# Second DFT in mirrored pairs, modulation rows in quadrants, shared check tiles: one change to a spectral mixing block with an MLP

## The chip, the cores and the metric

The kernel runs on one core of a Trainium2 chip. The metric is the device time of one execution in microseconds, as the median of several runs. The core has a matrix engine (PE, with a separate row PEld for the loading of weights), a vector engine (DVE), a scalar engine (ACT), a general engine (POOL) and an engine that only issues transfers (SP). Transfers can be issued by SP or by POOL; each of these queues issues in order, and an issue may wait for a semaphore.

## The reference

`x` is 2048 tokens of 1024 features. Six rows of 1024 numbers, `sa, ca, ga, sb, cb, gb`, come from one product of `silu(c)` with `w_mod` (1024 × 6144), and modulate two blocks:

```python
h = _layernorm(x) * (1 + ca) + sa
a, b = h @ hid_re.T, h @ hid_im.T             # first DFT, over the 1024 features
x = x + ga * (seq_re @ a - seq_im @ b)        # second DFT, over the 2048 tokens
h = _layernorm(x) * (1 + cb) + sb
x = x + gb * (gelu(h @ w1 + b1) @ w2 + b2)    # MLP, 1024 -> 3584 -> 1024
```

The four DFT matrices are inputs. All is float32.

## The kernel before

The kernel assumes that the DFT matrices have the symmetries of a DFT, works with folded (even and odd) sums and small parts of the matrices, and checks the assumption while it runs: all of both pairs of matrices is read, compared with itself mirrored or shifted, and the squares of the differences are summed. A verdict comes near the end; if it is bad, a general version runs after the fast one. Large products are done in float16, each operand split into a high and a low part, with three passes (high·high, high·low, low·high).

The program is written by a planner. Work is handed to it as tasks in named streams, each with an engine, an estimated cost, keys that it needs and a due time. The planner keeps a modelled clock for every engine and picks, among the tasks at the heads of the streams, by due time and by which can start first. So the order of an engine's instructions follows from costs and due times, and a changed cost may move work far away. The stages are:

- Modulation (`mod_part` and what follows, lines 2538 to 2598). Two of the six rows, `sa` and `ca`, are needed first. The eight pieces of `w_mod` are loaded by SP (L2504). Pieces 0, 1, 3 and 5 are multiplied on PE with a broadcast column of `silu(c)`, so that every output partition holds the row (L2556, four banks of 512); pieces 2, 4, 6 and 7 are multiplied and added on DVE (L2540, L2542) and reduced by four last PE products. DVE takes the largest value of each bank (L2568), ACT copies the row (L2582), PE turns it into columns by products with a 1 × 1 operand (L2588), and DVE scales these (L2592).
- The first LayerNorm (BN_STATS L2646, ACT L2676) on 16 tiles of 128 tokens, transposes on PE (L2693), and sums and differences of mirrored features (L2706, L2710, L2711, L2761 to L2788).
- The four remaining rows (`row`, L2900): per row 16 products of 128 × 512, broadcast to all output partitions. Rows `ga`, `cb` and `sb` come during the folds, `gb` late, in the stage of the second LayerNorm.
- First DFT (L2969), then the second DFT in `seq_tile(i)` for 16 tiles of 128 tokens: a product Q of 12 or 13 matmuls of 512 columns (L3058), a product P of 24 or 26 of 256 or 257 columns (L3046), a copy of Q by ACT (L3063), and `P - Q` and `P + Q` for the lower and upper columns by DVE (L3068, L3073). Tiles 4 to 7 of each half use negated copies of two parts of the matrix (`neg_tasks`, ACT L3015).
- Second LayerNorm in pairs of tiles (`ln2(b)`, b = 0 to 7). For b = 0, 6 and 7 `x` is loaded beside (L3101) and added by DVE (L3138, L3139); for b = 1 to 5 an accumulating transfer of POOL adds `x` (L3145) to what DVE made (L3143). The sum is stored (L3148), squared by ACT, and the reciprocal root taken by ACT (L2620) and DVE (L2626 to L2629); two scalings by DVE (L3158, L3162), a shift by DVE (L3169) and ACT (L3171). Then PE transposes (`turn`, L3181), ACT copies the result into a single buffer (L3185), and the pieces of `z` (L3211, L3220, L3233) become the first MLP operand.
- The MLP: products of the first layer (L3628) and the second (L3742). Groups of 12 products of the first two blocks (`gemm3_first`) are put into gaps of PE before the last transposes. The checks run beside the MLP: loads by POOL (L3559, with lists of rows L3552), differences by DVE (L3542), squares by ACT (L3533).

Weights `w1` and `w2` are also folded and split by DVE and ACT (L2379, L2391, L2405) and stored to memory in float16 (for `w1`'s first three blocks by POOL); loads of `fw` bring them back.

## Time and profile before

| | us |
|---|---|
| three runs | 1371.27, 1367.63, 1370.13 |
| median | 1370.13 |
| span of the profiled execution | 1368.1 |
| PE busy in the span | 1285.2 |
| DVE busy | 1089.1 |
| ACT busy | 748.2 |
| POOL busy | 263.8 |

The profile is of one execution, and its span lies within the three runs. Busy shares are means over the whole span; the stages above have different limits, so the prediction reads them by stretches of time. In a row of the timeline stand start, length, engine and line, operation, output and input, and in brackets the idle time before and what ended it. In a group of instructions stand the count, the busy time, the mean in ns, and the idle time just before them.

### The profile page before, as it was taken

The numbers are of one execution on the slowest core, as the hardware profiler recorded it, in microseconds if no ns is written. First come the engines' busy times: TensorE is split into PE (matmuls) and PEld (weight loads), VectorE is DVE, ScalarE is ACT, GpSimd is POOL, SyncE is SP. The second block draws the span as 40 slices with busy tenths as digits, with TensorE's granted clock in tenths as the row PEclk, the third lists the DMA queues.
The fourth block names the chain that finished last, engine by engine and source line by source line (L and its number), as shares of the span: only waits on it lengthen the run. The fifth ranks groups of instructions, "written<-read, shape, count | busy, mean of one in ns | idle before, by whom it ended". The sixth has DMA issues, their size and how long they took to land.

```text
span 1368.1 us, 17330 instructions
## 1 busy us (share of the span) xinstructions
PE 1285.2 (94%) x6081; PEld 620.1 (45%) x6081; DVE 1089.1 (80%) x1623; ACT 748.2 (55%) x1188; POOL 263.8 (19%) x426
## 2 busy tenths in 40 slices
...
GB/s 367 335 249 210 1 171 168 146 196 341 245 150 217 261 197 228 181 228 157 158 173 139 193 246 193 283 338 351 244 320 233 300 268 294 264 307 235 175 80 112
DMA packets 109753, 306.21 MB, mean 224 GB/s; under 512 B 14076, under 2 KB 14076, under 8 KB 107736
## 3 DMA queue, kind: packets, MB, share of 16 engines
...
q8 instruction: 49, 0.80, 0.2%
...
## 4 chain that ended last, share of the span: by engine, by line
PE 67%; DVE 10%; DMA 3%; ACT 2%; issue 2%; SPq 1%; POOL 0%; DVEq 0%; POOLq 0%; ACTq 0%
PE ps L3742 34%; PE ps L3628 31%; DVE arena L2391 2%; DVE arena L3220 1%; DVE arena L3162 1%; DVE arena L2405 1%; ACT arena L2379 1%; DMA arena<-in_w_dram 1%; PE ps L3046 1%; DVE arena L3233 1%; DMA arena<-in_wm_dram 1%; PE ps L3058 1%; DMA frow_gbb<-arena 0%; DVE arena L3654 0%; PE ps L3181 0%
## 5 line engine op out<-in xcount | busy, mean ns | idle before, releaser
L3628 PE MATMUL ps<-arena 128*128 128x512 f16 x2352 | 515.1, 381 | 9.7 <-DMA arena<-fw 5.4
L3742 PE MATMUL ps<-arena 128*128 128x512 f16 x2352 | 510.7, 379 | 4.9 <-DVE arena L3792 4.2
L3628 PEld LDWEIGHTS <-arena 128*128 128x128 f16 x2352 | 230.8, 98 | 290.2 <-issue 9.6
L3742 PEld LDWEIGHTS <-arena 128*128 128x128 f16 x2352 | 229.8, 98 | 283.5 <-DVE arena L3792 3.2
L3792 DVE SCALAR_TENSOR_TENSOR arena<-ps,i4c,arena 128x1024 f32<-128x1024 f32 x179 | 229.4, 1282 | 103.0 <-PE ps L3742 101.0
L2379 ACT ACTIVATE arena<-arena,shc 128x512 f16<-128x512 f32 (+1 forms) x115 | 116.0, 1017 | 134.4 <-DVE arena L2405 81.5
L2405 DVE TENSOR_TENSOR arena<-arena 128x512 f32<-128x512 f32 (+1 forms) x196 | 148.9, 764 | 3.7
L2391 DVE SCALAR_TENSOR_TENSOR arena<-arena,shc 128x512 f16<-128x512 f32 (+1 forms) x115 | 128.8, 1121 | 28.2 <-ACT arena L2379 27.8
L3533 ACT ACTIVATE arena<-arena 128x512 f32<-128x512 f32 (+5 forms) x148 | 91.2, 617 | 108.7 <-DVE arena L3542 89.8
L3647 ACT ACTIVATE arena<-arena,b1s,i1c 128x512 f32<-128x512 f32 x78 | 63.5, 814 | 94.4 <-DVE arena L3654 94.4
L3654 DVE TENSOR_TENSOR arena<-arena,ps 128x512 f32<-128x512 f32 x78 | 53.4, 685 | 51.6 <-PE ps L3628 50.9
L2379 ACT ACTIVATE arena<-arena,s1c 128x512 f16<-128x512 f32 (+1 forms) x70 | 60.7, 885 | 56.9 <-DVE arena L2405 39.6
L3542 DVE TENSOR_TENSOR arena<-arena 128x256 f32<-128x256 f32 x240 | 87.9, 420 | 1.8 <-DMA arena<-in_cre_dram 1.8
...
L3559 POOL DMA_DIRECT2D arena<-in_cim_dram x99 | 54.5, 551 | 92.3 <-ACT arena L3533 86.4
L2391 DVE SCALAR_TENSOR_TENSOR arena<-arena,s1c 128x512 f16<-128x512 f32 (+1 forms) x70 | 65.7, 958 | 2.9 <-ACT arena L2379 2.8
L3559 POOL DMA_DIRECT2D arena<-in_cre_dram x99 | 54.6, 552 | 68.3 <-ACT arena L3533 51.5
L3650 ACT ACTIVATE arena<-ps 128x512 f32<-128x512 f32 x78 | 45.9, 589 | 37.5 <-PE ps L3628 37.3
L2900 PE MATMUL ps<-arena,scol 128*128 128x512 f32 x128 | 61.5, 630 | 2.7 <-DMA arena<-in_wm_dram 2.4
L2391 DVE SCALAR_TENSOR_TENSOR arena<-arena,s2c 128x1024 f16<-128x1024 f32 x49 | 61.8, 1278 | 1.0 <-ACT arena L2379 1.0
L3046 PE MATMUL ps<-arena 128*128 128x256 f16 (+3 forms) x400 | 50.5, 286 | 10.1 <-DVE arena L3073 10.1
L3311 ACT ACTIVATE ps<-arena 128x1024 f32<-128x1024 f32 x46 | 46.7, 1016 | 19.0 <-DMA arena<-in_w_dram 9.6
...
## 6 DMA issues: line engine op xcount, KB each, us to landing
fw<-arena SPq DMA_DIRECT2D x71, 512.0 KB, 5.1
arena<-fw SPq DMA_DIRECT2D x119, 256.0 KB, 5.0
arena<-fw SPq DMA_DIRECT2D x49, 512.0 KB, 6.2
arena<-in_cre_dram POOLq DMA_DIRECT2D x96, 256.0 KB, 5.5
arena<-in_cim_dram POOLq DMA_DIRECT2D x96, 256.0 KB, 5.3
arena<-in_wm_dram SPq DMA_DIRECT2D x32, 512.0 KB, 6.8
arena<-in_w_dram SPq DMA_DIRECT2D x32, 512.0 KB, 6.2
arena<-in_w_dram SPq DMA_DIRECT2D x56, 256.0 KB, 4.7
```

Of the source, the lines that this page charges most:

```text
L2379: act.activation(o[m][0], q(j), AF.Copy, **sc)
L2391: dve.scalar_tensor_tensor(o[m][1], q(j), scale, o[m][0], op0=ALU.mult, op1=ALU.subtract)
L2405: dve.tensor_tensor(q(d), q(a), q(b), op=op)
L2900: pe.matmul(bank((6 if n < 3 else 4) + h), scol[:, k : k + 1].to_broadcast([P, P]), FA(o + 512 * h, (1, 512)), start=k == 0, stop=k == 7,)
L3046: pe.matmul(PA(pb + o, (1, w)), l, r, start=n == 0, stop=n == len(mm_) - 1)
L3533: f = lambda: act.activation(sq(a), sq(a), AF.Square, accum_out=csum[0:pn, n : n + 1])
L3542: dve.tensor_tensor(a[:, o::2], a[:, o::2], b[:, o::2], op=op)
L3559: return lambda t: gp.dma_start(t[0:pn], v)
L3628: pe.matmul(ps.rearrange("p (k t) -> p k t", k=4), w1c[:, m, s, a, d * P : (d + 1) * P], zc(m)[:, b, :, d, :], start=(start and d == 0 and ...
L3647: act.activation(dst, src, AF.Gelu_apprx_tanh, scale=inv, bias=b1s[:, 2 * p + j : 2 * p + j + 1])
L3742: pe.matmul(t[:, j], hidc[:, c_, m, a, k * P : (k + 1) * P], w2c[:, m, c_, w], start=(start and c_ == 0 and n == 0), stop=(c_ == 1 and n = ...
L3792: lambda: dve.scalar_tensor_tensor(dst, ps[b], inv, dst, op0=ALU.mult, op1=ALU.add), kp[b],
```

## The change

It does six things.

- Second DFT: `seq_pair(b)` takes the place of two `seq_tile`s. One P and one Q give both tiles of a pair, since a mirrored token has the same real row read backwards in the features. `up` is 257 columns wide, and LN2 reads the second tile through `yr`, an access with negative step. Only the tile with token 0 needs a further product of one output row (26 matmuls) and three ACT copies. `neg_tasks` is gone. The tokens of the second tile are the mirrored ones, so they are loaded, added and stored with lists of rows (`mirrored`, `from_rows`, `to_rows`, all on POOL): one load each for b = 0, 6 and 7, five accumulating loads, eight stores, four accumulating stores at the end.
- Modulation rows in quadrants: the products for the first rows write 32 output partitions each, four pieces of 512 columns at four places of the same bank, for all eight pieces of `w_mod`. DVE's multiply-adds are gone, one maximum and an all-reduce on POOL take the place of four maxima, four transposes that of 34 small products. The rows of `row` become 16 quarter products, a copy and two products that sum the quarters. `gb` is made in the middle of the second DFT, not late.
- x tiles 4 to 7 are loaded ahead of the eight pieces of `w_mod`.
- A second buffer for the transposed tiles (`ZT0`), used in turn until b = 5.
- The first MLP products and some weight loads wait for other keys (`zlo`, P and Q of earlier pairs).
- Checks share tiles (`fetch`, `chk`): a tile that is compared several times is loaded once; 76 fewer transfers of 256 KB. Differences, squares and the verdict stay.

The core of the diff:

```diff
+    def mirrored(v, h, k):
+
+        return v[0:1024], bass.IndirectOffsetOnAxis(ap=idx_m[:, 4 * h + k : 4 * h + k + 1], axis=0)
+
+    def last_rows(blk, r, hf):
+
+        c_ = slice(512 * hf, 512 * hf + 512)
+        return [o_s[1, 3 - 2 * blk - j if r else 4 + 2 * blk + j, :, c_] for j in range(2)]
+
+    def from_rows(dst, rows, idx, **op):
+        gp.indirect_dma_start(out=dst, out_offset=None, in_=rows, in_offset=idx, **op)
+
+    def to_rows(rows, idx, src, **op):
+        gp.indirect_dma_start(out=rows, out_offset=idx, in_=src, in_offset=None, **op)
...
     for i in range(4):
         load_x(i)
     load_raw1(0)
+    for i in range(4, 8):
+        load_x(i)
     for k in range(8):
         load(("wm", k), lambda k=k: sp.dma_start(wm2(k), wm[:, k, 0 : 2 * D]), cost=2.75)
-    for i in range(4, 8):
...
-        if k in (2, 4, 6, 7):
...
+            if k == 0:
+                for q in (2, 3):
+                    pe.matmul(quarter(VB, q, 512), ones[0:1, 0:32], ones[0:1, :], start=True, stop=False)
+            for q in range(4):
+                pe.matmul(
+                    quarter(VB, q, 512), scol[:, k : k + 1].to_broadcast([P, 32]), wm2(k)[:, 512 * q : 512 * q + 512],
+                    start=k == 0 and q < 2, stop=k == 7,
+                )
+
+        add("modp", "pe", CP * (1 + (k == 0)), f, [("wm", k)], ("mp", k), 1.0)
...
+                    for q, o in enumerate(places):
+                        pe.matmul(
+                            quarter(6 * 512 + 512 * h, q, 512),
+                            scol[:, 4 * c_ + q : 4 * c_ + q + 1].to_broadcast([P, 32]), FA(o + 512 * h, (1, 512)),
+                            start=c_ == 0, stop=c_ == 1,
+                        )
+
+            deps = list(ls)
+            if c_ == 0:
+                deps += [("rowe", n - 1)] if n else ["mod"]
+            add("rowp", "pe", 2 * CP, f, deps, ("wrr", m), due)
+
+        def whole():
+            for h in range(2):
+                pe.matmul(
+                    bank(6 + h), part[:, 0:1].to_broadcast([P, P]), FA(o_ + 512 * h, (1, 512)),
+                    start=True, stop=True,
+                )
+
...
-    def seq_tile(i):
-        tp, ti = divmod(i, 8)
...
+    def seq_pair(b):
+        tp, ti = divmod(b, 4)
+        kk = 128 * ti
+        due = 75.0 + 22.0 * b
...
+
+        def p_mm(bank_=pb, left=left, m=P):
...
+        add("seqp", "pe", 2.75, q_mm, ak[tp] + copk + bank_deps + ([("qs", b - 2)] if b > 1 else []), ("Q", b), due)
+        add("seqp", "pe", 3.0, p_mm, ak[tp] + copk + bank_deps + ([("y", b - 2)] if b > 1 else []) + ([("y1", 0)] if b == 1 else []), ("P", b), due)
...
 
         def up():
             dve.tensor_tensor(
-                FA(y + 512, (1, 2), (2, 256)), PA(pb + 511, (256, 2), (-1, 256)), qv(i, 256, (256, 2), (-1, 256)), op=ALU.add
+                FA(y + 512, (1, 2), (2, 257)), PA(pb + 511, (256, 2), (-1, 257)), qv(b, 256, (256, 2), (-1, 257)), op=ALU.add
             )
...
+        if b == 0:
...
+            def one(t, a, ch):
+                return HA(NEG + 2 * a + ch - 2, (1, 1)) if ch > 1 else HA(cop(0, 0, a, ch), (1, 1))
+
+            r = add("seqp", "pe", 3.0, lambda: p_mm(1024, one, 1), [k, *ak[0], *copk, *bank_deps], None, due)
+
+            def whole():
+                act.activation(FA(y + 1024, (1, 1024)), FA(y + 1024, (-1, 1024)), AF.Copy)
+
+            def row_():
+                act.activation(FA(y + 1024, (1, 2), (2, 256), pn=1), PA(1024 + 255, (257, 2), (1, 256), pn=1), AF.Copy)
+                act.activation(FA(y + 1536, (1, 2), (2, 256), pn=1), PA(1024 + 511, (256, 2), (-1, 256), pn=1), AF.Copy)
+
+            k = add("seqn", "act", 1.05, whole, [("y", 0)], None, due)
+            add("seqn", "act", 1.2, row_, [k, r], ("y1", 0), due)
...
     def load_xw(b):
-        f = lambda: sp.dma_start(wb(b), x_s[b // 4, 2 * b % 8 : 2 * b % 8 + 2].rearrange("r p e -> p r e"))
-        load(("xw", b), f, w_free(b), cost=2.8, stream="xw", due=70.0)
+        h, k = divmod(b, 4)
+        f = lambda: sp.dma_start(wb(b)[:, 0], x_s[h, 4 + k])
+        load(("xw", b, 0), f, w_free(b), cost=1.4, stream="xw", due=70.0)
+        f = lambda: from_rows(wb(b)[:, 1], *mirrored(x_r, h, k))
+        load(("xw", b, 1), f, w_free(b), cost=1.4, stream="xw", due=70.0)
...
+        x1 = {}
         wfree = w_free(b)
-        for n in range(2):
+        h, k_ = divmod(b, 4)
+        yr = FA(YW[b][0] + 1024, (-1, 1024))
+        for n in (1, 0):
             i = 2 * b + n
+            src = yr if n and b else y[:, n]
+            have = [("y1", 0) if n and not b else ("y", b)]
             if b in ADDED:
...
                     y[:, n], y[:, n], 1.0, w[:, n], op0=ALU.mult, op1=ALU.add, accum_out=su[:, n : n + 1]))
             else:
-                last[0] = None
-                k = step("dve", 1.32, lambda n=n: dve.scalar_tensor_tensor(
-                    y[:, n], y[:, n], 1.0, ga_t, op0=ALU.mult, op1=ALU.mult, accum_out=su[:, n : n + 1]), [("y", i), *rows])
-                store("xa", i, lambda n=n, i=i: gp.dma_start(y[:, n], x_s[i // 8, i % 8], accum_op=ALU.add), k)
+                k = step("dve", 1.32, lambda n=n, src=src: dve.scalar_tensor_tensor(
+                    y[:, n], src, 1.0, ga_t, op0=ALU.mult, op1=ALU.mult, accum_out=su[:, n : n + 1]), [*have, *rows])
+                if n:
+                    f = lambda: from_rows(y[:, 1], *mirrored(x_r, h, k_), compute_op=ALU.add)
+                else:
+                    f = lambda: gp.dma_start(y[:, 0], x_s[h, 4 + k_], accum_op=ALU.add)
+                store("xa", i, f, k)
                 k = "st", "xa", i
-            x1.append(k)
-            store("x1", i, lambda n=n, i=i: sp.dma_start(o_s[i // 8, i % 8], y[:, n]), k)
+            x1[n] = k
+            if n:
...
+        def ev():
+            if n and b > 3:
+                v = zt(b, n).rearrange("p (d t) -> p d t", t=P)
+                act.activation(v, PA(6 * 512 + P - 1, (P, ND), (-1, P)), AF.Copy)
+            else:
+                act.activation(zt(b, n), ps, AF.Copy)
+
+        deps = [("turn", i)] + ([(b - (2 if b < 7 else 1), "zlo", ms) for ms in ((0, 1), (3, 4), (2, 5), (6,))] if b > 1 else [*hidend, ("y1", 0)])
+        add("zte", "act", 1.1, ev, deps, ("zt", i), due)
 
```

How the change moves instructions is seen at three places.

First, DVE at the end of the modulation. `scol` is `silu(c)`, `s1c` a scale of `w1`, `mx` and `m` the maxima, `mcol` the columns of the row. Before:

```order
L2542 SCALAR_TENSOR_TENSOR arena_65<-arena_65,scol_105 128x2048
L2391 SCALAR_TENSOR_TENSOR arena_65<-arena_65,s1c_147 128x2x512
L2542 SCALAR_TENSOR_TENSOR arena_65<-arena_65,scol_105 128x2048
L2646 BN_STATS xst_19_139<-arena_65 128x6 x2
L2647 BN_AGGR csum_136<-xst_19_139 128x2
L2568 TENSOR_REDUCE mx_107<-ps 128x1 x4
L2571 TENSOR_REDUCE m_3_98<-mx_107 128x1
L2158 TENSOR_SCALAR m_3_98<-m_3_98 128x1
L2573 RECIPROCAL m_3_98<-m_3_98 128x1
L2574 TENSOR_SCALAR m_3_98<-m_3_98 128x1
L2575 TENSOR_SCALAR m_3_98<-m_3_98 128x1
L2646 BN_STATS xst_20_140<-arena_65 128x6 x2
```

After:

```order
L2408 SCALAR_TENSOR_TENSOR arena_65<-arena_65,s1c_161 128x512
L2408 SCALAR_TENSOR_TENSOR arena_65<-arena_65,s1c_161 128x2x512
L2575 TENSOR_REDUCE mx_111<-ps 128x1
L2579 TENSOR_SCALAR vspec_112<-ps,sel_113 128x2 x2
L2582 TENSOR_SCALAR m_4_99<-mx_111 128x1
L2175 TENSOR_SCALAR m_4_99<-m_4_99 128x1
L2584 RECIPROCAL m_4_99<-m_4_99 128x1
L2585 TENSOR_SCALAR m_4_99<-m_4_99 128x1
L2597 TENSOR_SCALAR mcol_114<-ps,m_4_99 128x16
L2600 TENSOR_SCALAR msp_115<-ps,m_4_99 4x2
L2601 TENSOR_SCALAR mneg_116<-mcol_114 128x4
L2602 TENSOR_TENSOR mbias_117<-mcol_114 128x2
```

The four passes over pieces of `w_mod` are gone (three earlier ones stand above the part shown), so are three of four maxima, and no statistics of x (BN_STATS) stand between the maximum and `mcol`.

Second, POOL's queue from the stores of folded `w1` (`fw_1`, `fw_2`) to the middle of the second DFT. `idxm` is the list of mirrored rows. Before:

```order
L3423 DMA fw_1_77<-arena_65 128x1024
L3423 DMA fw_1_77<-arena_65 128x2048
L3423 DMA fw_2_78<-arena_65 128x2048
L3423 DMA fw_2_78<-arena_65 128x1024
L3423 DMA fw_2_78<-arena_65 128x2048
L3145 DMA arena_65<-in_x_dram 128x1024 x10
L3226 DMA fzc_67<-arena_65 256x1x512
L3226 DMA fzc_68<-arena_65 256x1x512
```

After:

```order
L3501 DMA fw_1_77<-arena_65 128x1024
L3501 DMA fw_1_77<-arena_65 128x2048
L2168 DMA arena_65<-in_x_dram,idxm_98 128x1024
L3501 DMA fw_2_78<-arena_65 128x2048
L3501 DMA fw_2_78<-arena_65 128x1024
L2171 DMA out_dram<-arena_65,idxm_98 1024x1024
L3501 DMA fw_2_78<-arena_65 128x2048
L2943 DMA frow_gb<-arena_65 128x1024
L2948 DMA frow_gbb<-arena_65 128x1024
L2168 DMA arena_65<-in_x_dram,idxm_98 128x1024
L3212 DMA arena_65<-in_x_dram 128x1024
L2168 DMA arena_65<-in_x_dram,idxm_98 128x1024
```

Where ten plain accumulating loads stood in a row, mirrored loads, mirrored stores, plain accumulating loads and the two stores of `gb` alternate; the first mirrored load stands behind the stores of `fw_1`. The store of a mirrored tile is on POOL now, and was on SP.

Third, ACT near the last two transposes. L3185 (before) and L3261, L3259 (after) copy transposed tiles; L3928 and L4051 copy products of the first MLP blocks. Before:

```order
L3924 ACTIVATE arena_65<-ps,b1s_144,i1c_148 128x512
L3211 ACTIVATE arena_65<-arena_65 128x2x512
L3928 ACTIVATE arena_65<-ps 128x512
L2379 ACTIVATE arena_65<-arena_65,shc_149 128x2x512
L3211 ACTIVATE arena_65<-arena_65 128x512
L3924 ACTIVATE arena_65<-arena_65,b1s_144,i1c_148 128x512
L3928 ACTIVATE arena_65<-ps 128x512
L3185 ACTIVATE arena_65<-ps 128x1024
L3928 ACTIVATE arena_65<-ps 128x512
L3185 ACTIVATE arena_65<-ps 128x1024
L2379 ACTIVATE arena_65<-arena_65,shc_149 128x2x512
```

After:

```order
L4047 ACTIVATE arena_65<-arena_65,b1s_158,i1c_162 128x512
L4047 ACTIVATE arena_65<-ps,b1s_158,i1c_162 128x512
L3290 ACTIVATE arena_65<-arena_65 128x512
L2396 ACTIVATE arena_65<-arena_65,shc_163 128x2x512
L4051 ACTIVATE arena_65<-ps 128x512
L3261 ACTIVATE arena_65<-ps 128x1024
L3259 ACTIVATE arena_65<-ps 128x1024
L4047 ACTIVATE arena_65<-arena_65,b1s_158,i1c_162 128x512
L4051 ACTIVATE arena_65<-ps 128x512
L2396 ACTIVATE arena_65<-arena_65,shc_163 128x2x512
L2396 ACTIVATE arena_65<-arena_65,s2c_165 128x2x512
```

Before, five copies of first-layer products stood ahead of the first of the last two tiles; after, there are four. In PE's order the matmuls of the first layer ahead of the last pair's transposes are 84 before and 60 after. The last tile is copied reversed, by L3259.

491 lines of the change are left out of this document (260 added, 231 removed).

## Prediction

> **What bounds the kernel now.** I read the page first: its busy totals, and the shares of the chain that ended last.
>
> ```profile
> PE 1285.2 (94%) x6081; PEld 620.1 (45%) x6081; DVE 1089.1 (80%) x1623; ACT 748.2 (55%) x1188; POOL 263.8 (19%) x426
> PE 67%; DVE 10%; DMA 3%; ACT 2%; issue 2%; SPq 1%; POOL 0%; DVEq 0%; POOLq 0%; ACTq 0%
> ```
>
> PE leads, but 94% is a mean over stages. I therefore cut the span where the work changes: the modulation row is ready, the first DFT starts, the first LN2 operation, the last LN2 scale, the first second-layer product.
>
> ```profile
> core 0: us, PE busy (x) PEld busy (x) DVE busy (x) ACT busy (x) POOL busy (x), PEclk, DMA share, GB/s
> 0.00:46.50 46.50, 29.12 (x96) 14.86 (x96) 29.50 (x59) 21.51 (x38) 9.99 (x27) 0.96 0.95 378
> 46.50:115.40 68.90, 52.52 (x192) 32.30 (x193) 57.66 (x98) 52.40 (x88) 0.40 (x1) 0.85 0.80 269
> 115.40:194.30 78.90, 72.08 (x420) 39.80 (x418) 65.00 (x89) 44.19 (x57) 6.83 (x13) 0.91 0.29 92
> 194.30:351.50 157.20, 130.18 (x737) 79.51 (x736) 138.08 (x248) 116.19 (x181) 21.11 (x29) 0.90 0.71 220
> 351.50:393.00 41.50, 39.43 (x191) 18.60 (x190) 32.24 (x37) 30.84 (x39) 4.04 (x6) 1.00 0.43 166
> 393.00:1368.10 975.10, 961.87 (x4453) 435.08 (x4451) 766.66 (x1098) 483.10 (x789) 221.42 (x350) 1.00 0.69 227
> ```
>
> The last row holds 71% of the time, and there PE idles 13 of 975 us: the two MLP products set it. The change adds no product to it and takes DMAs from POOL, so I carry it over at 975.1. The time is decided before 393. In the fifth row PE is the bound again (39.4 of 41.5). In the fourth, DVE works 138 of 157 us and PE 130, and PE's waits look back at DVE; in the second DVE is at 58 of 69. The first is a DMA stage, at 0.95 of the queues' time.
>
> **Modulation (first row).** The order of its end, with the last transfer at the top:
>
> ```profile
> 15.75 3.50 PE L2556 MATMUL ps<-arena,scol 128*128 128x512 f32 x4 [15.75 <-DMA arena<-in_wm_dram]
> 35.89 2.35 DVE L2542 SCALAR_TENSOR_TENSOR arena<-arena,scol 128x2048 f32<-128x2048 f32 x1
> 38.29 3.70 PE L2556 MATMUL ps<-arena 128*128 128x512 f32 x8 [1.14 <-DVE arena L2542]
> 44.27 1.94 PE L2588 MATMUL ps<-arena 1*128 1x1 f32 x16
> 46.37 0.23 DVE L2592 TENSOR_SCALAR mcol<-ps,m 128x16 f32<-128x16 f32 x1 [1.39 <-PE ps L2589]
> ```
>
> The change puts four x tiles ahead of the eight w_mod loads. Four tiles are 2.1 MB, at the row's 378 GB/s 5.5 us. All that must have landed by then is 4 x tiles, 4 quarter-MB loads of w1, 4 more x tiles and 8.4 MB of w_mod, 13.6 MB: 36 us, plus a microsecond to start, 37. Behind it stand one group of four quarter products, the maximum, its reduction on POOL, two short copies, four transposes and the scale. The nearest rows are 0.6 to 0.7 us for a product or a maximum and 0.2 for the scale; with a handover each I take 6 us. So 43 against 46.5: **−3.5**. Bounds: 40 and 48, if each step waits a full microsecond.
>
> **Rows and folds (second row).** The modulation rows are full-width float32 products now:
>
> ```profile
> L2556 PE MATMUL ps<-arena,scol 128*128 128x512 f32 x32 | 17.5, 695 | 15.7 <-DMA arena<-in_wm_dram 15.7
> L2900 PE MATMUL ps<-arena,scol 128*128 128x512 f32 x64 | 29.9, 626 | 2.7 <-DMA arena<-in_wm_dram 2.4 <-ACT arena L2915 0.3
> L2900 PE MATMUL ps<-arena,scol 128*128 128x512 f32 x32 | 15.6, 615 | 0.0
> ```
>
> The second line is this stage, the third the next one. A row is 16 products, 10 us. Changed, it is 16 products of 32 output partitions, four of them side by side if the quadrants run together, so 4 × 0.63, and two full ones: 3.8 us. No trace here has a quadrant; the bounds for one group of four are 0.63 (together) and 2.5 (one after another). I take together, since the four write different output partitions and use different columns of the array. [...]
>
> PE loses 22 us of its 52.5 here, but DVE has 57.7 of 68.9 us of work which is all kept, so at most its 11.2 idle us can go. Some of that idle is behind PE's queue, some behind ACT's copies. I take half: **−5.3**. Bounds 0 and −11.
>
> **First DFT and first pair (third row).** PE is busy 72 of 79; the 15.6 us of rows become 3.8, and row 3's 3.8 comes in between the first products: −8. What ends the stage is the first LN2 operation on x:
>
> ```profile
> 157.13 22.18 PE L2969 MATMUL ps<-arena 128*128 128x257 f16 x130 [2.39 <-DVE arena L2788]
> 180.73 2.76 PE L3058 MATMUL ps<-arena 128*128 128x512 f16 x12 [1.42 <-DVE arena L2530]
> 194.33 1.22 DVE L3138 TENSOR_TENSOR arena<-arena 128x1024 f32<-128x1024 f32 x1
> ```
>
> After the change that operation takes the mirrored tile first, and its x comes by an indirect load that stands on POOL behind the w1 stores of group 1 (the second place in the order above). Until those have landed it can't be issued, so I let half of the 8 us pass: **−4**. Bounds +3 and −9.
>
> **Second DFT and LN2 (fourth row).** These are the groups that halve, and what DVE waits for:
>
> ```profile
> L3046 PE MATMUL ps<-arena 128*128 128x256 f16 (+3 forms) x400 | 50.5, 286 | 10.1 <-DVE arena L3073 10.1
> L3058 PE MATMUL ps<-arena 128*128 128x512 f16 (+1 forms) x200 | 46.0, 379 | 1.4 <-DVE arena L2530 1.4
> L3068 DVE TENSOR_TENSOR arena<-ps,arena 128x512 f32<-128x512 f32 x16 | 11.0, 685 | 0.0
> L3073 DVE TENSOR_TENSOR arena<-ps,arena 128x512 f32<-128x512 f32 x16 | 11.0, 685 | 0.0
> L3015 ACT ACTIVATE arena<-arena 128x1024 f16<-128x1024 f16 x8 | 8.1, 1044 | 0.0
> DVE lns L2626 <- ACT lns L2620: 10.7, 5, 6.8
> DVE arena L3139 <- DMA arena<-in_x_dram: 0.9, 1, 0.9
> PE ps L3046 <- DVE arena L3073: 10.1, 3, 6.6
> ```
>
> PE loses 48 us of products and gains 26 one-row ones (at most 26 × 0.29 = 7). That is off the path: DVE bounds. DVE loses 14 of the 28 evictions that lie in this stage, at 0.685: −9.6; the row sums' b2 product (1.2) and work that came earlier from the w1 tasks (about 1.3) are added: 138.1 − 7.1 = 131. Reading a tile backwards I cost at nothing, because the same lines already read PSUM backwards: L3073 does, L3068 does not, and both take 685. DVE's idle is 19.1 us, of which 10.7 is one kind, the root from ACT, with one wait of 6.8; PE's own waits on the evictions add up to 10.1. ACT loses the 8 negations and 8 of 16 copies at 0.6: 13 of 116 us. Products come early now, which should take a third of the idle; 13 left. 131 + 13 = 144: **−13**. Bounds: −26 with no idle, and −7 with the idle kept and growing.
>
> **The end of LN2 (fifth row).** Early products of the first layer fill PE's gaps:
>
> ```profile
> 320.93 5.29 PE L3628 MATMUL ps<-arena 128*128 128x512 f16 x12 [3.87 <-DMA arena<-fw]
> 341.29 2.76 PE L3628 MATMUL ps<-arena 128*128 128x512 f16 x12 [1.50 <-DMA arena<-fw]
> 353.86 5.34 PE L3628 MATMUL ps<-arena 128*128 128x512 f16 x24
> 366.22 1.04 PE L3181 MATMUL ps<-ident,arena 128*128 128x128 f32 x8
> 367.09 26.06 PE L3628 MATMUL ps<-arena 128*128 128x512 f16 x120
> ```
>
> Of 252 such matmuls, 84 stand ahead of the last pair's transposes; in the changed order 60 do (the third place above). Two groups of 12 at 2.67 (5.34 for 24) go to the tail: **+5.3**. Bounds: 0, if the idle they left is used otherwise, and +8.
>
> **The checks and doubled z buffer.** Fewer POOL loads beside the MLP: nothing, since PE covers it (13 us idle at most). The second z buffer is in the idle of ACT and PE already counted.
>
> The sum: 1368.1 − 3.5 − 5.3 − 4 − 13 + 5.3 = 1347.6. The median stands at 1370.1 beside this execution's 1368.1, so I add half of that difference and predict **1348.5**.
>
> **Rivals.**
> *DVE closes up.* The same steps, but idle goes: in the second row another 5, in the fourth another 13: 1330. For it: PE's waits at L3046 have to shrink when products halve. Against: the LN2 chain DVE, ACT, DVE remains serial. Chance 0.15.
>
> *The quadrants run one after another*, the change not doing what it says. A group of four costs 2.5; a row is 16 × 0.63 + 1.3 = 11.3 instead of 10, and nothing is won in rows two and three (+9.3); row 3 falls into the second DFT, whose PE has room. [...] Chance 0.12.
>
> *Late first-layer products.* They now wait for z of an earlier pair and for weights that follow P and Q; two more groups of 12 in the tail and a weight wait as at 320.93 (3.87): +9, 1357. Against: DMA share there should fall. Chance 0.08.
>
> *POOL becomes the bound: slower.* Tokens of mirrored tiles go out and in by indirect transfers. The rows near to them:
>
> ```profile
> arena<-in_x_dram POOLq DMA_DIRECT2D x10, 512.0 KB, 5.7
> arena<-in_cim_dram POOLq DMA_DIRECT2D x96, 256.0 KB, 5.3
> L3552 POOL DMA_INDIRECT arena<-in_cim_dram,idxs x16 | 18.2, 1140 | 4.8 <-issue 3.9 <-DVE arena L3542 0.9
> L3145 POOL DMA_DIRECT2D arena<-in_x_dram x10 | 8.7, 867 | 72.0 <-DVE arena L3143 36.6 <-DVE lns L2626 19.7 <-DVE lns L3152 9.5
> ```
>
> An indirect issue costs 1.1 us against the plain one's 0.87, so 16 of them are at most 18 us of POOL, which has 136 idle in the fourth row. But POOL issues in order (the second place again): the store of a mirrored tile waits on its gather-add, and the next gather-add, then the next plain one, stand behind it. Per pair that is two landings in series, 11.4 at 5.7 us; a pair has 144/8 = 18 us. From a landing of 9 us the queue sets the pace. At 15 us five gather-adds cost 5 × (30 − 18) = 60, of which the three sets of LN2 buffers hide about 20: 1348 + 40 = 1388. For it: an indirect row moves 4 KB a token at strides; against: the indirect check loads are issued and landed in step with the direct ones. [...] Chance 0.10.
>
> **Numbers.** The forecast has 0.55 with its own range 1338 to 1357. 1330 (0.15) and 1357 (0.08) widen it, and 1365 borders on it: 1328 to 1366 leaves about 2 in 10 out. About 0.3%, 4 us, is what a measurement can tell from no change. Faster: 0.55 + 0.15 + 0.08 + most of 0.12 = 0.84; same: 0.06; slower 0.10.
>
> **What would show it.** The scale of the modulation near 43; four L2564 quarter products starting within one's length of another; the first DFT near 106, the first LN2 operation near 181; the last LN2 scale near 325; landing of the indirect x loads under 9 us and POOL waits shorter than DVE's; a second layer starting near 372 and 975 us after that. I am wrong if the stage after the first DFT takes as long as before, if DVE waits on in_x_dram for more than a few us in sum, or if the MLP's 975 changes by more than 5.

## The result, and the profile after

The changed kernel takes 1351.82 us (median of four runs, 1349.98 to 1354.39), the kernel before 1370.7 beside it (1367.63 to 1371.62). The ratio is 0.9857, with a 95% interval of 0.984 to 0.9874. The profiled execution of the changed kernel has a span of 1347.9 us against 1368.1, so 20.2 us less.

The busy totals of the changed kernel and the shares of its chain that ended last, from the page:

```profile
PE 1209.9 (90%) x5825; PEld 569.3 (42%) x5825; DVE 1080.5 (80%) x1624; ACT 746.4 (55%) x1198; POOL 253.0 (19%) x380
PE 66%; DVE 10%; issue 9%; DMA 8%; ACT 5%; POOL 1%; SPq 0%; DVEq 0%; POOLq 0%; ACTq 0%
```

PE has lost 75 us of work and the span 20. So most of what the change takes from PE was not worth its length, and the question is where it went. The changed kernel, cut at the prediction's events (columns as in the prediction's table of stretches):

```profile
0.00:45.16 45.16, 17.96 (x91) 4.58 (x92) 23.40 (x63) 23.23 (x41) 9.97 (x41) 0.89 0.96 379
45.16:106.44 61.28, 40.71 (x209) 21.58 (x209) 56.21 (x90) 52.01 (x83) 0.36 (x1) 0.77 0.85 277
106.44:178.58 72.14, 62.90 (x438) 35.44 (x437) 60.82 (x86) 41.02 (x55) 5.68 (x11) 0.91 0.52 184
178.58:327.00 148.42, 77.77 (x414) 49.63 (x412) 130.98 (x231) 109.07 (x171) 44.12 (x43) 0.73 0.70 208
327.00:375.48 48.48, 48.48 (x230) 22.74 (x228) 37.76 (x46) 35.96 (x44) 4.36 (x7) 0.98 0.45 160
375.48:1347.90 972.42, 962.07 (x4453) 435.36 (x4451) 771.35 (x1113) 485.10 (x808) 188.48 (x279) 1.00 0.64 205
```

The first cut is the start of the modulation's scale, behind which DVE's next operation starts at 45.3; the cut at 327.00 lies 0.8 us ahead of the last LN2 scale, which stands at 327.80. With 45.3 and 327.80 the stages answer the prediction's sum as follows:

| stage | before | after | moved | forecast |
|---|---|---|---|---|
| modulation | 46.5 | 45.3 | −1.2 | −3.5 |
| rows and folds, to the first DFT | 68.9 | 61.1 | −7.8 | −5.3 |
| first DFT, to the first LN2 operation | 78.9 | 72.1 | −6.8 | −4 |
| to the last LN2 scale | 157.2 | 149.2 | −8.0 | −13 |
| to the first second-layer product | 41.5 | 47.7 | +6.2 | +5.3 |
| MLP to the end | 975.1 | 972.4 | −2.7 | 0 |
| sum | 1368.1 | 1347.9 | −20.2 | −20.5 |

The sum is nearly right, its terms less so: six errors of 0.9 to 5.0 us cancel. A cut at the second DFT's own products says more than these stages do. Here is the kernel before, from its first product of the second DFT (180.73) to the first LN2 transposes (214.58), to the first transposes of the last pair, those of tile 14 (352.93), and to the first second-layer product (392.99):

```profile
180.73:214.58 33.85, 33.02 (x228) 21.95 (x228) 30.27 (x55) 17.82 (x29) 5.09 (x9) 1.00 0.55 174
214.58:352.93 138.35, 111.93 (x600) 66.43 (x600) 121.29 (x216) 108.54 (x166) 18.81 (x26) 0.89 0.74 229
352.93:392.99 40.06, 38.22 (x184) 18.25 (x185) 30.80 (x35) 29.40 (x37) 4.04 (x6) 1.00 0.41 160
```

And the changed kernel between the same four events:

```profile
162.26:202.94 40.68, 33.55 (x228) 19.46 (x227) 33.26 (x64) 20.12 (x31) 12.38 (x17) 1.00 0.58 210
202.94:332.29 129.35, 63.83 (x307) 40.77 (x308) 113.19 (x201) 103.66 (x157) 35.83 (x35) 0.68 0.75 223
332.29:375.48 43.19, 43.19 (x210) 20.58 (x209) 37.02 (x40) 30.72 (x38) 3.55 (x5) 1.00 0.39 135
162.26:375.48 213.22, 140.56 (x743) 80.81 (x743) 183.47 (x304) 154.51 (x225) 51.77 (x56) 0.81 0.65 203
```

This is the main finding. The first product of the second DFT starts 18.5 us earlier (162.26 for 180.73). From there to the second layer it takes 213.2 us where it took 212.3, though PE works 140.6 us there and not 183.2. Between the two traces, the halved second DFT has won nothing net in the place where it was halved; all of the gain ahead of the MLP had been won before its first product. The three stretches are +6.8, −9.0 and +3.1. (The run with x behind w_mod, below, shows that a start of that product some us later can be made good further on, so this is where the gain stands and not yet why.)

DVE's work in that place is the same too: 183.5 us after, 182.4 before (30.27 + 121.29 + 30.80). Its largest groups that differ, in the kernel before, are the two evictions L3068 and L3073, 11.0 us each, whose lines stand in the prediction, and the folding of weights (L2391 and L2405 are steps of it):

```profile
L2405 DVE TENSOR_TENSOR arena<-arena 128x512 f32<-128x512 f32 (+1 forms) x16 | 12.6, 789 | 0.3
L2391 DVE SCALAR_TENSOR_TENSOR arena<-arena,shc 128x1024 f16<-128x1024 f32 (+1 forms) x8 | 9.1, 1146 | 0.1
L2391 DVE SCALAR_TENSOR_TENSOR arena<-arena,s1c 128x512 f16<-128x512 f32 (+1 forms) x6 | 6.1, 1012 | 1.3 <-ACT arena L2379 1.3
L2391 DVE SCALAR_TENSOR_TENSOR arena<-arena,s2c 128x1024 f16<-128x1024 f32 x4 | 5.1, 1279 | 0.0
```

and the same steps in the changed kernel, where L3099 and L3104 are the evictions and L2408 and L2422 the folding:

```profile
L2422 DVE TENSOR_TENSOR arena<-arena 128x512 f32<-128x512 f32 (+1 forms) x20 | 15.9, 796 | 0.5
L2408 DVE SCALAR_TENSOR_TENSOR arena<-arena,shc 128x1024 f16<-128x1024 f32 (+1 forms) x8 | 9.2, 1150 | 1.7 <-ACT arena L2396 1.6
L2408 DVE SCALAR_TENSOR_TENSOR arena<-arena,s2c 128x1024 f16<-128x1024 f32 x7 | 9.0, 1279 | 0.2 <-ACT arena L2396 0.2
L2408 DVE SCALAR_TENSOR_TENSOR arena<-arena,s1c 128x1024 f16<-128x1024 f32 (+1 forms) x8 | 7.9, 1011 | 1.2 <-ACT arena L2396 1.2
L3099 DVE TENSOR_TENSOR arena<-ps,arena 128x512 f32<-128x512 f32 x8 | 5.5, 687 | 0.0
L3104 DVE TENSOR_TENSOR arena<-ps,arena 128x514 f32<-128x514 f32 x8 | 5.5, 686 | 0.0
```

The evictions fell from 22.0 to 11.0, as forecast. Folding rose from 32.9 to 42.0. It doesn't lie where the evictions lay: ahead of the first transposes it is 13.4 us where it was 9.5, in the tail 28.6 where it was 23.4, and in the middle there is none in either kernel. That more of it falls behind the first product because the stages ahead got shorter is likely, but no run shows it. Reading a tile backwards costs nothing: of the ten products with `ga` at L3207 five read their tile backwards through `yr`, and their mean is 1225 ns where the same ten took 1220 forward (L3143 before).

Five rows of PE's timeline after, and one of DVE's, show how the other parts came out (start, length, instruction, count, and in brackets the wait):

```profile
30.76 1.06 PE L2564 MATMUL ps<-arena,scol 128*32 128x512 f32 x8 [1.42 <-DMA arena<-in_wm_dram]
40.55 1.94 PE L2564 MATMUL ps<-arena,scol 128*32 128x512 f32 x8 [1.76 <-DMA arena<-in_wm_dram]
128.20 3.64 PE L2913 MATMUL ps<-arena,scol 128*32 128x512 f32 x32
202.94 1.97 PE L3252 MATMUL ps<-ident,arena 128*128 128x128 f32 x8 [5.13 <-ACT arena L3242]
325.16 7.29 PE L3735 MATMUL ps<-arena 128*128 128x512 f16 x24 [10.06 <-DMA arena<-fw]
```

```profile
185.04 1.23 DVE L3204 SCALAR_TENSOR_TENSOR arena<-arena 128x1024 f32<-128x1024 f32 x1 [5.24 <-DMA arena<-in_x_dram,idxm]
```

Eight records are one group of four quarter products (a float32 product makes two records here: the 64 products of L2900 were 128). Four full ones took 3.70 us in the kernel before (its row at 38.29), a group of quarters takes 1.06 (the row at 30.76), both at a granted clock of 1.00: the quadrants do run side by side. The last w_mod piece is multiplied at 40.55, not 37. The wait of 10.06 us for weights at 325 is new, that of 5.24 us for the first mirrored tile of x was 0.89, and PE waits 5.13 us for ACT's shift (L3242) before the first transposes, where it waited 0.83.

### The profile page after: what moved, and what is told of

Read it like the earlier page. It is cut to its first block, busy times and chain, and to the rows that moved or that the text cites. A ratio compares the mean times of both kernels' runs of the same rounds, so it can differ in the third digit from the quotient of the medians.

```text
span 1347.9 us, 16675 instructions
## 1 busy us (share of the span) xinstructions
PE 1209.9 (90%) x5825; PEld 569.3 (42%) x5825; DVE 1080.5 (80%) x1624; ACT 746.4 (55%) x1198; POOL 253.0 (19%) x380
## 4 chain that ended last, share of the span: by engine, by line
PE 66%; DVE 10%; issue 9%; DMA 8%; ACT 5%; POOL 1%; SPq 0%; DVEq 0%; POOLq 0%; ACTq 0%
PE ps L3849 31%; PE ps L3735 31%; DMA arena<-in_wm_dram 2%; DMA arena<-in_x_dram 2%; DMA out_dram<-arena,idxm 1%; PE ps L3252 1%; DVE arena L3899 1%; DVE arena L2408 1%; ACT arena L3181 1%; PE ps L3014 1%; ACT arena L2396 1%; DVE arena L3233 1%; DVE arena L2549 1%; DMA arena<-in_cre_dram 1%; DVE arena L2774 1%
## 5 line engine op out<-in xcount | busy, mean ns | idle before, releaser
L3735 PE MATMUL ps<-arena 128*128 128x512 f16 x2352 | 515.3, 381 | 15.7 <-DMA arena<-fw 10.1
L3735 PEld LDWEIGHTS <-arena 128*128 128x128 f16 x2352 | 231.1, 98 | 296.2 <-issue 12.2
L3619 ACT ACTIVATE arena<-arena 128x512 f32<-128x512 f32 (+4 forms) x159 | 97.5, 615 | 108.2 <-DVE arena L3628 85.8
L2408 DVE SCALAR_TENSOR_TENSOR arena<-arena,shc 128x512 f16<-128x512 f32 (+1 forms) x115 | 128.9, 1122 | 34.2 <-ACT arena L2396 33.8
L2422 DVE TENSOR_TENSOR arena<-arena 128x512 f32<-128x512 f32 (+1 forms) x196 | 149.0, 765 | 3.9
L2408 DVE SCALAR_TENSOR_TENSOR arena<-arena,s1c 128x512 f16<-128x512 f32 (+1 forms) x70 | 65.8, 959 | 5.3 <-ACT arena L2396 5.0
L3252 PE MATMUL ps<-ident,arena 128*128 128x128 f32 x128 | 25.1, 361 | 45.9 <-ACT arena L3242 37.3
L2408 DVE SCALAR_TENSOR_TENSOR arena<-arena,s2c 128x1024 f16<-128x1024 f32 x49 | 62.2, 1280 | 1.3 <-ACT arena L2396 1.3
L2396 ACT ACTIVATE arena<-arena,s2c 128x1024 f16<-128x1024 f32 x49 | 55.2, 1140 | 3.3 <-DVE s2c L3418 1.8
L3014 PE MATMUL ps<-arena 128*128 128x256 f16 (+5 forms) x297 | 43.3, 293 | 6.4 <-ACT arena L2793 3.2
L3181 ACT ACTIVATE arena<-arena,lns 128x1024 f32<-128x1024 f32 x32 | 36.5, 1142 | 21.0 <-DMA arena<-in_x_dram 9.3
```

The lines of the kernel that those rows point to most:

```text
L2396: act.activation(o[m][0], q(j), AF.Copy, **sc)
L2408: dve.scalar_tensor_tensor(o[m][1], q(j), scale, o[m][0], op0=ALU.mult, op1=ALU.subtract)
L2422: dve.tensor_tensor(q(d), q(a), q(b), op=op)
L3014: pe.matmul(PA(bp + o, (1, w), pn=m), l, r, start=i == 0, stop=i == len(mm_) - 1)
L3181: act.activation(junk[:, n], src[:, n], AF.Square, scale=scale, bias=bias[:, n : n + 1], accum_out=v[:, n : n + 1])
L3619: f = lambda: act.activation(v, v, AF.Square, accum_out=csum[0:pn, n : n + 1])
```

## The experiments

Theory ahead of the runs: the gain is that of the quadrants and of DVE's lost evictions; products of the second DFT are off the path. Rivals: PE's halved products are themselves the gain; the new wait for weights at 325 eats part of it; lists of rows burden POOL. Each kernel below is the changed one with one edit. All were timed in rounds with the kernel before, and each ratio is against that; differences between kernels are between medians (the changed kernel 1351.82) and spans (1347.9). The kernel before had medians of 1370.6 to 1372.9 in these rounds, so a difference of 2 to 3 us between two medians is not a finding by itself; stretches of the traces say more.

### The quadrants

**Later rows without quadrants.** The four later rows are 16 full products and one copy again.

```diff
-                            quarter(6 * 512 + 512 * h, q, 512),
-                            scol[:, 4 * c_ + q : 4 * c_ + q + 1].to_broadcast([P, 32]), FA(o + 512 * h, (1, 512)),
-                            start=c_ == 0, stop=c_ == 1,
+                            bank(6 + h),
+                            scol[:, 4 * c_ + q : 4 * c_ + q + 1].to_broadcast([P, P]), FA(o + 512 * h, (1, 512)),
+                            start=c_ == 0 and q == 0, stop=c_ == 1 and q == 3,
...
-        k = add("rowa", "act", 1.1, lambda: act.activation(r, src, AF.Copy), [("wrr", 2 * n + 1), *free], None, due)
-        k = add("rowp", "pe", 2 * FP, whole, [k], None, due)
```

> The four later modulation rows are made as before the change, 16 products of 128 output partitions each and one copy, and all else stays changed. If the quadrants bring the gain ahead of the first DFT (61.3 us from the modulation to the first DFT where it was 68.9, 72.1 to the first LN2 operation where it was 78.9), both stages go back by 5 to 14 us in sum and the time is 1357 to 1366. If the earlier x tiles and the shorter chain of the first rows bring it, and PE only had room there, the time stays within 3 us of 1351.8.

Measured: 1360.32, ratio 0.9919 (0.9895 to 0.9943), 8.5 us above the changed kernel. The first DFT starts only 1.2 us later (107.68), but it takes 63.2 us instead of 55.8 to the first product of the second; 2.9 more are lost from there to the second layer (11.0 in all on the span, 8.5 on the median). In the midst of the first DFT stands, in PE's timeline:

```profile
130.35 14.00 PE L2914 MATMUL ps<-arena,scol 128*128 128x512 f32 x32
```

where the changed kernel has 3.64 at 128.20 and two whole products, 1.98 together. So a row on the path of the first DFT is worth nearly its PE time, 8.4 us, of which 7.3 shows; the rows under the folds, where DVE sets the pace, are worth about 1.

**First rows without quadrants.** The modulation multiplies four pieces on DVE again; the order of x and w_mod stays the new one. In this kernel and the next, the loads for the first of the later rows also wait for the modulation again, as they did before the change. (In both, the row `gb*b2` is stored after its place has been used again, so the constant that it adds to all tokens is another one; work and transfers are the same.)

```diff
+            m = FA(MACC, (1, 2048))
...
+                    dve.tensor_scalar(m, wm2(k), scol[:, k : k + 1], None, op0=ALU.mult)
...
+                    dve.scalar_tensor_tensor(m, wm2(k), scol[:, k : k + 1], m, op0=ALU.mult, op1=ALU.add)
...
-                pe.matmul(
-                    quarter(VB, q, 512), scol[:, k : k + 1].to_broadcast([P, 32]), wm2(k)[:, 512 * q : 512 * q + 512],
-                    start=k == 0 and q < 2, stop=k == 7,
-                )
```

> The first two modulation rows are made as before the change (four pieces of w_mod on DVE, four banks, four maxima, 34 small products for the columns), all else stays changed, the x tiles' earlier load too. DVE's work up to the first DFT was 87.2 us before and is 79.6 after. If DVE sets the pace up to there, the first DFT goes from 106.4 back to 113 to 116 and the time to 1359 to 1362. If the shorter chain behind the last piece of w_mod is not what counts and another part of the change brought these 9 us, the time stays within 3 us of 1351.8.

Measured: 1365.24, ratio 0.9957 (0.9942 to 0.9973): 13.4 us above. The scale of the modulation is at 56.1, 10.8 us later, the first DFT starts 9.9 later, and 6.5 more are lost from the first product of the second DFT to the first transposes (47.2 for 40.7). From DVE's timeline of this run:

```profile
40.32 4.73 DVE L2561 SCALAR_TENSOR_TENSOR arena<-arena,scol 128x2048 f32<-128x2048 f32 x2
```

The last two pieces are multiplied from 40.32 to 45.05 on DVE, and the four maxima and the two rows of small products follow in series. That is later than the 46.5 of the kernel before; x tiles 4 to 7, which are loaded first here, are likely a part of it (5 us in the run with x behind w_mod, below). The old form with the old order of loads beside the new second DFT was not tried, so how the 13.4 us divide between the quadrants and the order under the old form stays open.

**Both undone.**

> Both kinds of modulation rows are made as before (the first two as in the run above, the later four as in the run with full-width rows), all else stays changed, so that the second DFT in pairs, the buffers, the shared checks and the x order are left alone. If the quadrants bring nearly all and the second DFT in pairs brings next to nothing, because what it saves is spent up to its first transposes and at the tail, the sum of the two undone parts is 16 to 19 us and the time 1366 to 1372, as before the change. If the second DFT in pairs brings its forecast 8 us net of the tail, it is 1358 to 1364.

The edit is the two above together. Measured: 1365.93, ratio 0.996 (0.9945 to 0.9974), 14.1 us above the changed kernel. The two single prices, 8.5 and 13.4, don't add up. The first product of the second DFT starts at 178.53, so of the 18.5 us by which it had moved up 16.3 are gone: that gain is the quadrants'. What is left, about 5 us on the median and 2 on the span, is the second DFT in pairs with the checks, the buffers and the new order of x. The second and third stretch of this run between the four events:

```profile
216.13:342.25 126.12, 70.25 (x334) 44.60 (x335) 112.28 (x203) 97.44 (x152) 34.05 (x31) 0.69 0.71 206
342.25:394.13 51.88, 50.47 (x233) 23.83 (x234) 41.65 (x53) 38.59 (x48) 7.51 (x12) 0.97 0.53 188
```

Here too the middle is 12.2 us shorter than before the change (126.1 for 138.3) and the tail gives 11.8 back (51.9 for 40.1): the second layer starts at 394.13, where it started at 392.99 before the change. So without the quadrants nothing is won ahead of the MLP; the MLP itself takes 971.8 us for 975.1, which is the price of the checks (below). The order of x stays the new one here, and the modulation comes 8 us later than before the change (54.3 for 46.4), so the pairs were not measured quite alone.

**x behind w_mod.**

```diff
-    for i in range(4, 8):
-        load_x(i)
     for k in range(8):
         load(("wm", k), lambda k=k: sp.dma_start(wm2(k), wm[:, k, 0 : 2 * D]), cost=2.75)
+    for i in range(4, 8):
+        load_x(i)
```

> x tiles 4 to 7 are loaded behind the eight pieces of w_mod again; all else stays changed. If that order brings the gain ahead of the first DFT, the modulation comes some 5 us earlier (40 instead of 45.2), but the first DFT 5 or more later than 106.4, and the time is 1357 or more. If the quadrants bring it, the first DFT is within 2 us of 106 or earlier, and the time within 4 us of 1351.8.

Measured: 1350.45, ratio 0.9844 (0.982 to 0.9867), not to be told from the changed kernel. The modulation is ready at 40.3, 5 us earlier, and the first DFT starts at 105.9 instead of 106.4: between them DVE has folds and LayerNorm to do in any order. So the moment at which the modulation is ready hardly matters in the new form. But the first DFT takes longer, and the first product of the second starts 5.6 us later (167.84), which hardly shows in the time either. The middle and the tail of this run:

```profile
206.13:327.08 120.95, 59.08 (x283) 39.71 (x283) 107.87 (x196) 97.28 (x151) 30.62 (x29) 0.66 0.71 208
327.08:378.50 51.42, 50.82 (x233) 24.03 (x233) 41.63 (x52) 38.59 (x48) 7.37 (x12) 0.96 0.56 194
```

The planner left 24 more matmuls of the first layer for the tail, which is 8.2 us longer, and the middle is 8.4 shorter; the second layer starts 3.0 later than in the changed kernel. An earlier first product is therefore not worth its length by itself.

### The halved second DFT

**Each product twice.** P and Q of all pairs are computed a second time into the same place, which gives PE back about what the change took.

```diff
-        add("seqp", "pe", 2.75, q_mm, ak[tp] + ...
-        add("seqp", "pe", 3.0, p_mm, ak[tp] + ...
+        add("seqp", "pe", 2.75, lambda: (q_mm(), q_mm()), ak[tp] + ...
+        add("seqp", "pe", 3.0, lambda: (p_mm(), p_mm()), ak[tp] + ...
```

> Each P and Q of the second DFT is computed twice into the same bank (300 more matmuls, some 48 us of PE), with DVE's and ACT's work and the order as in the changed kernel. If DVE and the chain through ACT set the pace of the LN2 stage, as the prediction has it, PE's 70 us of idle there take most of it: not over 1358, and the granted clock of that stage rises from 0.73. If the halved products themselves brought the gain of that stage (7.9 us), it goes, and PE's extra 48 us push the end of LN2 by 20 us or more: over 1370.

Measured: 1374.23, ratio 1.0012 (0.9999 to 1.0024): 22.4 us above the changed kernel. The theory that PE's idle would take most of it falls: PE works 39.8 us more in the place, and more than half of that shows. The first two stretches of this run:

```profile
163.12:221.06 57.94, 57.94 (x392) 35.54 (x392) 38.67 (x72) 21.29 (x31) 18.11 (x21) 1.00 0.62 189
221.06:356.45 135.39, 79.26 (x444) 50.14 (x443) 107.94 (x192) 102.72 (x156) 29.55 (x30) 0.76 0.63 196
```

Ahead of the first transposes PE has no idle at all, and the stretch grows from 40.7 to 57.9: PE gets 24.4 us more work there, 7.1 fit into its idle, and the other 17.3 show. The rows for the changed kernel's products there tell why so much stands in this place (PE's groups between 162.26 and 202.94):

```profile
L3078 PE MATMUL ps<-arena 128*128 128x257 f16 (+6 forms) x130 | 15.2, 272 | 2.0 <-ACT arena L3136 2.0
L3090 PE MATMUL ps<-arena 128*128 128x512 f16 (+1 forms) x61 | 14.1, 379 | 0.8 <-DVE arena L2549 0.8
L2913 PE MATMUL ps<-arena,scol 128*32 128x512 f32 x32 | 3.8, 598 | 0.0
L2926 PE MATMUL ps<-arena,part 128*128 128x512 f32 x4 | 1.9, 592 | 0.0
```

Sixty-one matmuls of Q are five pairs; with P of four pairs and the one-row product they are 29.3 us, and there is the row `gb`, 5.7 us, all of which PE's order puts ahead of the first transposes. Before the change it was six tiles there:

```profile
L3046 PE MATMUL ps<-arena 128*128 128x257 f16 (+3 forms) x156 | 18.2, 272 | 0.0
L3058 PE MATMUL ps<-arena 128*128 128x512 f16 x72 | 16.6, 379 | 1.4 <-DVE arena L2530 1.4
```

34.8 us. So the planner filled the place won by the pairs with more pairs and with `gb`, and PE's work ahead of the first transposes is 33.6 us after and 33.0 before. Behind the first transposes the doubled products add only 6.0 us: there PE has room. The run says how much slack PE has in this order, 7.1 us ahead of the first transposes; it does not say that PE sets them. In the changed kernel PE is done with the fifth Q at 197.8 and waits for ACT's shift, so what makes the stretch 6.8 longer is the chain of DVE and ACT up to that shift. It has two parts. From the first product to the first LN2 operation pass 16.3 us where 13.6 did (DVE folds 2.6 us more up to there), and from there to the first transposes 24.4 where 20.3 did, with 5.24 us of waiting for x where 0.89 were.

**DVE's evictions twice.** DVE gets 11.0 us of work back.

```diff
-        add("yev", "dve", 0.72, low, deps, None, due)
-        add("yev", "dve", 0.72, up, deps, ("y", b), due)
+        add("yev", "dve", 0.72, lambda: (low(), low()), deps, None, due)
+        add("yev", "dve", 0.72, lambda: (up(), up()), deps, ("y", b), due)
```

> Each of DVE's two evictions of a pair is done twice (16 more of 0.685 us, 11.0 us), with the order as in the changed kernel. If DVE sets the pace of the LN2 stage, most of it shows there: 1358 to 1363. If DVE has slack there (it is idle for some 18 of 148 us), and the chain through ACT and the weights behind the tail decide, the time is 1351 to 1355.

Measured: 1357.64, ratio 0.9911 (0.9876 to 0.9946): +5.8 on the median; the second layer starts 7.5 later. About half to two thirds of what DVE gets shows.

**DVE without the subtractions of z.** The 24 subtractions that combine the pieces of `z` are left out (so the first MLP operand is another), 20.8 us of DVE.

```diff
-            f = lambda: dve.tensor_tensor(q(*d), q(*a), q(*c), op=ALU.subtract)
+            f = lambda: None
```

> DVE's subtractions among the pieces of z (24 instructions, 20.8 us of DVE, 18.2 of them between the first product of the second DFT and the second MLP layer) are left out, so that z's pieces are not the reference's; ACT, PE, POOL, the transfers and the order of what is left are as in the changed kernel. If DVE's work is what fills that stretch (183.5 us of work in 213.2 us, where it was 182.4 in 212.3 before the change), a good half of it comes off: 1336 to 1343. If PE's backlog of first-layer products or the chain through ACT sets its length, the time is 1346 to 1352.

Measured: 1348.09, ratio 0.9821 (0.9796 to 0.9847): −3.7; the second layer starts 2.1 us earlier. So work added to DVE costs by more than half, and work taken away gives a tenth to a fifth. DVE's waits from 160 to 395 us in the changed kernel:

```profile
DVE lns L2633 <- ACT lns L2627: 4.1, 7, 1.5
DVE arena L3229 <- ACT arena L3181: 2.1, 2, 1.4
DVE arena L3299 <- ACT arena L3290: 1.5, 3, 1.0
```

and in this run:

```profile
DVE lns L2633 <- ACT lns L2627: 9.7, 11, 1.5
DVE arena L3229 <- ACT arena L3181: 6.8, 2, 3.6
DVE arena L3299 <- ACT arena L3290: 5.7, 5, 2.3
```

These three grew from 7.7 to 22.2 us, 14.5 of the 20.8: DVE now waits for ACT's root, square and z pieces. DVE is not a lone bound in this place. It and ACT hand each pair to and fro, and what DVE saves turns into waiting for ACT. Which instruction of ACT would have to be shortened was not tried.

**Folding of w1 earlier.** If DVE's folding behind 162 us is what fills the place of the evictions, then earlier due times for it should move it back.

```diff
-        push(f"wq{g}", "wq", w1_norm(g) + w1_tasks(g), (1.5, 80.0, 88.0)[g])
+        push(f"wq{g}", "wq", w1_norm(g) + w1_tasks(g), (1.5, 60.0, 66.0)[g])
```

> The folding of w1's second and third block gets due times 60 and 66 instead of 80 and 88, so that the planner puts a few of its DVE and ACT instructions ahead of the last evictions of the first DFT. If the first pair's eviction waits for that folding on DVE (172.8 us, 5 us behind its product), the first transposes come up to 4 us earlier and the time is 1347 to 1350. If the work is only moved in front of other DVE work that is needed as soon, it is within 2 us of 1351.8.

Measured: 1358.14, ratio 0.9905 (0.9881 to 0.9928): 6.3 us slower. The first DFT starts 1.2 later, the first transposes 2.1, those of tile 14 (turn 14) 6.1. The edit moved little: behind the first product 40.7 us of folding are left of 42.0. The middle is 4.0 us longer though DVE works 0.8 us less in it, and the wait that grew is the one of DVE (L2633) for ACT's root (L2627), 10.1 us in sum for 4.1, once 8.4. So the run shows what a changed order can cost, and doesn't settle what the folding costs.

### Buffers and the wait for weights

**One buffer for the transposed tiles.**

```diff
-    ... [17024, 4160] * 3 + [17024] * 2
+    ... [17024] * 8
...
-        deps = [("turn", i)] + ([(b - (2 if b < 7 else 1), "zlo", ms) ...] if b > 1 else [*hidend, ("y1", 0)])
+        deps = [("turn", i)] + ([(b - 1, "zlo", ms) ...] if b > 0 else [*hidend, ("y1", 0)])
```

> One buffer for the transposed tiles for all pairs, the weights' waits as in the changed kernel. If the second buffer brings part of the gain in the LN2 stage, each pair's first copy waits for z of the pair before, and the time is 1354 to 1362. If nothing waits there, it is within 3 us of 1351.8.

Measured: 1352.43, ratio 0.9874 (0.9844 to 0.9903): 0.6 on the median, 2.2 on the span. Turn 14 comes 5.0 later, but the tail is 40.7 for 43.2 and the second layer starts 2.5 later. The second buffer is worth nothing that these rounds can tell.

**Second buffer only up to b = 3.** Its place is then free earlier, and the loads of weights that follow it in memory no longer wait for z of pair 5, but of pair 3.

```diff
-    ... [17024, 4160] * 3 + [17024] * 2
+    ... [17024, 4160] * 2 + [17024] * 4
...
-        deps = [("turn", i)] + ([(b - (2 if b < 7 else 1), "zlo", ms) ...
+        deps = [("turn", i)] + ([(b - (2 if b < 5 else 1), "zlo", ms) ...
...
-    ... [("P", 3), ("Q", 3)] + [(5, "zlo", ms) ...
+    ... [("P", 3), ("Q", 3)] + [(3, "zlo", ms) ...
```

> The second buffer for z is used by pairs 1 and 3 only, not by pair 5, and the weights of the last three first-layer pieces, which lie in the same place, are loaded after z of pair 3 instead of pair 5. In the order 24 and 84 first-layer matmuls are left after the first and the second transposes of the last pair, where 48 and 144 are left in the changed kernel. If the 10.1 us for which PE waits on these weights, with what they push back, is what the tail costs, the second layer starts at 356 to 366 instead of 375.5 and the time is 1333 to 1343. If the tail is set by DVE's end of LN2 and by ACT, or pair 5 now waits for z of pair 4, the time is within 4 us of 1351.8.

Measured: 1356.0, ratio 0.9885 (0.986 to 0.9909): 4.2 us slower on the median, 7.2 on the span, and not 9 to 19 faster, as it should be if the wait for weights cost its length. That wait is gone and the tail is 35.1 us for 43.2. Turn 14 comes 6.3 us later, the second layer starts 1.7 earlier (373.75), and the stage behind it takes 981.3 us for 972.4:

```profile
373.75:1355.10 981.35, 965.06 (x4453) 435.83 (x4451) 778.99 (x1114) 488.00 (x810) 188.03 (x278) 0.99 0.64 205
```

PE now waits 6.7 us for ACT in the first layer instead of 10.1 for weights, and 4.9 for ACT again behind the first 24 matmuls of the second. An earlier start of the second layer is not by itself a gain. The changed kernel's own trace says what the wait of 10.06 us hides. ACT's first shift of the last pair:

```profile
328.46 1.23 ACT L3242 ACTIVATE arena<-arena,lns 128x1024 f32<-128x1024 f32 x1
```

It ends at 329.7, and turn 14, which needs it, starts at 332.29, right behind the products that had waited. So at most 2.6 of the 10.06 us lie ahead of turn 14; the rest covers work of DVE and ACT that has to end anyhow. In the run with x behind w_mod PE hardly waits for weights, and waits 11.83 us for ACT's shift ahead of turn 14 instead. Behind turn 14 PE has no idle, and in the changed kernel and eight of these runs, all but the four that change what is left for the tail, the tail is 43.2 us each time.

### Checks and lists of rows

**Checks as before.** Each check loads both its tiles again.

```diff
-    CB = (136, 138, 140, 142, 216, 218, *range(32, 48, 2))
+    CB = ((136, 138), (140, 142), (216, 218), (32, 34), (36, 38), (40, 42), (44, 46))
...
-        add("chkl", "st", 0.0, lambda: load(v), list(free), ("chka", n))
+        deps = [add("chkl", "st", 0.0, lambda: load_a(a), free, ("chka", n))]
+        if load_b is not None:
+            deps.append(add("chkl", "st", 0.0, lambda: load_b(b), free, ("chkb", n)))
```

> The checks of the DFT matrices load each tile anew, as before the change, 76 more loads of 256 KB on POOL, all else changed. If the shared tiles bring the 2.7 us by which the MLP stage is shorter, the time is 1353 to 1357. If PE covers the loads and the 2.7 us have another reason, it is within 2 us of 1351.8.

Measured: 1354.86, ratio 0.9871 (0.9847 to 0.9895): +3.0. The last stage of this run:

```profile
377.51:1353.60 976.09, 962.39 (x4453) 435.36 (x4451) 762.25 (x1093) 478.66 (x786) 227.84 (x354) 1.00 0.69 226
```

976.1 us for 972.4, with PE's work the same (962.4, 962.1) and POOL 39 us busier: fewer loads cut PE's idle from 13.7 to 10.3. On the whole time this is near what a measurement can tell; the stage is steadier. It takes 970.7 to 974.5 us in the ten other runs with shared tiles (the cut-short second buffer left out), 976.1 in this one, and 975.1 in the kernel before.

**Plain transfers for the mirrored tiles.** Tokens of mirrored tiles go in forward order by plain POOL transfers (so x is added to the wrong tokens).

```diff
-        gp.indirect_dma_start(out=dst, out_offset=None, in_=rows, in_offset=idx, **op)
+        gp.dma_start(dst, rows, **({"accum_op": op["compute_op"]} if op else {}))
...
-        gp.indirect_dma_start(out=rows, out_offset=idx, in_=src, in_offset=None, **op)
+        gp.dma_start(rows, src, **({"accum_op": op["compute_op"]} if op else {}))
```

> Tokens of the mirrored tiles are loaded, added and stored forward with plain transfers of POOL in place of lists of rows, so that these tokens' x is taken and put in the wrong order; all else is changed. If the lists of rows cost time (an issue of 1.0 to 2.3 us against 0.9, landings near 6 us, and 5.2 us for which DVE waits on the first of them), the time is 1344 to 1349. If POOL has room for them, it is within 2 us of 1351.8.

Measured: 1349.42, ratio 0.9827 (0.98 to 0.9855): −2.4 on the median, with spans of 1348.8 and 1347.9 in the other order. The ratios differ by 0.003, some 4 us, so lists of rows cost between nothing and 4 us. The loads in the changed kernel (POOL's group from the first product of the second DFT on):

```profile
L2168 POOL DMA_INDIRECT arena<-in_x_dram,idxm x8 | 13.8, 1722 | 40.2 <-PE ps L3252 17.8 <-DVE arena L3207 14.2 <-DMA fw<-arena 7.6
```

and in this run:

```profile
L2168 POOL DMA_DIRECT2D arena<-in_x_dram x8 | 6.0, 756 | 44.7 <-DVE arena L3207 19.2 <-issue 18.0 <-DMA fw<-arena 7.5
```

An issue of a list takes 1.72 us for 0.76, but POOL is busy 51.8 of 213 us in the whole place. Both wait some 7.5 us until a store of folded `w1` has landed, before the first mirrored tile of x can be issued. DVE waits 3.6 us for that tile here and 3.6 to 7.2 in the runs with lists (5.24 in the changed kernel), so most of that wait belongs to the store and not to the list. No run took it away.

## Why the prediction was right, and where not

The forecast was 1348.5 (range 1328 to 1366, own range 1338 to 1357), and 1351.82 lies in both ranges. Point by point, by its own steps:

- **Modulation, −3.5: −1.2.** The step that failed is the landing: "all that must have landed by then" was 13.6 MB, 37 us; the last piece's product starts at 40.55. Up to there the trace has moved 15.2 MB, 1.2 of them in POOL's queue, which stores folded `w1` then, so 1.6 MB went beside what was counted. The chain behind it was shorter than the 6 us taken: 4.6. PE had a granted clock of 0.50 in it (40.55 to 45.30; below). The run with x behind w_mod shows that nothing hangs on this term.
- **Rows and folds, −5.3: −7.8.** Right in direction and inside the bounds. The price of a row was misread: 0.63 us is the mean of one record, and a float32 product makes two. The quoted 15.6 us with 32 records are one row, not a row and a half of "16 products, 10 us"; in quadrants a row is 3.64 + 1.98, not 3.8, and the two rows of this stage take 14.0 + 5.7 at a granted clock of 0.77. So PE lost 11.8 us here and not 22. The mechanism was the one named, DVE's idle and not PE's work: it fell from 11.2 to 5.1 (61.28 − 56.21), half of it as taken; DVE's work, "all kept", fell by another 1.4 (57.66 to 56.21).
- **First DFT and first pair, −4: −6.8.** The 8 us of rows were right, and the run without quadrants prices one row here at 8.4. What failed is "I let half of the 8 us pass". The first LN2 operation is the product with `ga`, which needs no x; the wait for the mirrored tile, 5.24 us behind the w1 stores as described, comes one operation later (178.58, forecast 181) and lands in the next stage.
- **Second DFT and LN2, −13: −8.0.** DVE's work was forecast at 131 and measures 130.98 (to 327.00). What failed is the idle: 13 assumed, 17.4 measured. "Products come early now, which should take a third of the idle" holds for the kind named, the wait for ACT's root, 10.7 us before and 4.1 after; but the wait for the mirrored x is 5.2 where it was 0.9, and smaller waits for ACT grew by 3.8. And "that is off the path: DVE bounds" is only half right. Halved, the products are off it; but PE has no more than 7.1 us to spare ahead of the first transposes, and the doubled products cost 22.4. Nor does DVE bound alone: 20.8 us less of its work gave 3.7.
- **End of LN2, +5.3: +6.2.** Right in cause and size: 24 more matmuls, and PE without idle. The wait for weights that the rival *late first-layer products* described is there (10.06 us at 325), so in part it came true; its price did not, since at most 2.6 us of it lie ahead of turn 14.
- **MLP, 0: −2.7.** "Nothing, since PE covers it" failed by a small size: PE's idle of 13 us is not covered, and the shared check tiles took 3 of it.
- **The second z buffer, nothing:** held, by the run with one buffer.

Two of the signs of being wrong are near: from the second DFT's own first product to the second layer it does take as long as before, and DVE waits 5.24 us for x. The terms were off by +2.3, −2.5, −2.8, +5.0, +0.9 and −2.7 us; that these sum to 0.3 is luck.

Rivals: the quadrants one after another are out (1.06 us for 3.70). The 1365 on which the forecast's range borders puts some 7 us on top of the 9.3 of that rival; no run shows such a term, and what the trace shows is 1.06 us for a group and 3.64 + 1.98 for a row. POOL as the bound is out (plain transfers give 4 us at most), though an issue of a list costs 1.72 us and not 1.1. DVE closing up did not come.

Where the halving went, then, as far as shown: its 43 us of PE work lie in three stretches. Ahead of the first transposes PE's work is no less, since the order put five pairs and `gb` where six tiles were; but PE waits at the end of it, and what makes the stretch longer, +6.8, is the late x and DVE's path to the first LN2 operation. In the middle DVE lost 8 us of work and the stretch 9.0. In the tail PE has no idle at all, and first-layer products that used to fill gaps stand there: +3.1. Where a run changes what is left for the tail (both undone, x behind w_mod, one buffer, the second buffer cut short), the middle and the tail trade, and what one wins the other mostly loses. That the sum of work on DVE and ACT sets the middle fits these runs, but no run varied ACT alone and none took the wait for x away, so how the +6.8 and the middle divide stays open. So does a rival: nine of the middle's fourteen tiles are transposed in 1.97 us and not 1.04 (last section), between two steps of ACT.
